# Attention and top-1 experts in one kernel: a new order for the first and last pairs of heads and the first expert block, and probabilities kept in two tiles

## The chip, the cores and the metric

The kernel runs on one core of a Trainium2 chip. The metric is the device time of one execution in microseconds. The profile is one profiled execution of the program. Engines are called as in the profile: PE is the matrix engine TensorE, PEld its weight loads, DVE is VectorE, ACT is ScalarE, POOL is GpSimd, and SP is the queue that issues most transfers.

## The reference

Attention over 8 batches of 8 heads, 576 tokens of 64 elements, with rotary embedding of q and k; its output, 4608 rows of 512, goes through a layer of eight experts of which each row uses one:

```python
scores = scale * np.matmul(q_rot, k_rot.transpose(0, 1, 3, 2))
scores = scores - np.max(scores, axis=-1, keepdims=True)
attn = np.exp(scores)
attn = attn / (np.sum(attn, axis=-1, keepdims=True) + 1e-09)
return np.matmul(attn, v).astype(np.float32)
...
x = np.ascontiguousarray(attn_out.transpose(0, 2, 1, 3)).reshape(B * S, H * D)
...
logits = x @ w_gate + modality_bias[modality_id]
e_idx = np.argmax(logits, axis=1)
...
gate_w = probs[np.arange(N), e_idx]
for e in range(E):
    mask = e_idx == e
    h = np.maximum(x[mask] @ w1[e], 0.0)
    out[mask] = gate_w[mask, None] * (h @ w2[e])
```

The experts' weights are 512 x 1024 and 1024 x 512, all in float32.

## The kernel before

**Attention.** The 64 heads are worked off as 32 pairs, four pairs to a batch. The steps of a pair are small jobs, and each has a name. T1, T2, R and LO are the rotary products (function `rope_`, L428 to L436, on POOL from the third pair on; HI, between R and LO, is a copy on ACT); SWH and SWL are transfers that swap the halves of partitions (L444, on SP). S0 to S8 are the scores on PE (L459), MN0 to MN8 the row extremes on DVE (L468), EX0 to EX8 the exponentials on ACT (L477), which write the probabilities. F0 to F3, FA and FB turn the probabilities over on PE (`fill`, L482), and A_ and B_ copy the result out of PSUM on ACT and DVE (`evac`, L419 and L516) into PH, and the tails of the sequence into PD. AVA and AVB multiply with v (L542): AVA for queries 0 to 255, AVB for queries 256 to 575. OTA and OTB copy that to SBUF, OUT multiplies with the gate's weights and turns it back (L577), and EVA and EVB (L589, L591, L593, on DVE) scale by the reciprocal row sum and write the rows X, the gate's logits G and the last 64 tokens XT. RE and RI prepare that reciprocal.

**Routing.** After each fourth pair BIAS, XO (the batch's rows go to DRAM) and fifteen steps RK0 to RK14 find each row's expert and its place in a table, and SC0 to SC4 write these places by indirect transfers from POOL (L694, `TAB<-VAL,oi`). A first plan (`plan0`, nine steps on POOL and DVE) assigns eight blocks of 256 rows from the first five batches alone, so that the experts' work can begin before attention is through.

**Experts.** For a block, SP reads the plan's values and the table (`ix`, `xi`), POOL works out addresses (L948) and issues eight indirect gathers (L956, `XG<-X,iy`), each of 128 rows of 128 elements. There are two buffers: even blocks use XG[0], odd blocks XG[1]. DVE transposes the rows (L1001, "tr"), ACT and DVE split them into a high and a low part in HL ("te"). The weights come by SP into staging buffers ST, and ACT (L419, W1H, W2H) and DVE (L416, W1L, W2L) split them in the same way ("hi", "lo"; "w1n", "hi2" and "lo2" are W1 for block 1). The first layer ("l1", L1020) is four groups of 24 matmuls, each of which fills one PSUM tile of half a slot; ACT (L1029, SW) and DVE (L1030, HX) read them ("l1e"). The second layer is L1043, ACT scales it (L1046), and POOL scatters it to the output (L1048).

**What sets the order.** Every job has a number. It is KEYS[name] + 14.438 x pair number, unless the table EDGE has an entry for that pair and name; jobs of the first expert block have theirs in the table MOE, relative to the last pair. All jobs are sorted by it, and the instructions of each engine and of SP's queue then run in exactly that order. Slot numbers for PSUM tiles (SLOTS) are fixed by name. From number 25 behind the last pair on, the expert blocks follow in a fixed program: block 0's second layer, block 1's first layer and so on, with the last batch's routing and the second plan woven in. The table AFTER adds waits ("place") to single gathers: gathers 3 to 7 of slot 0 wait for pair 30's AV or OUT, and all eight of slot 1 for slot 0's first layer. Waits between instructions otherwise follow from the tiles that they read and write; a PSUM tile of two halves counts as one.

Of the kernel before, what the change touches and what calls it, by code (L numbers as in the profile page):

```python
# [8 lines left out]
F32 = mybir.dt.float32  # L9
# [9 lines left out]
P = 128  # L19
# [43 lines left out]
        -329.744, "AVA": -327.201, "OTA": -302.117, "F3": -299.875, "A_F3": -295.073, "B_F3": -294.953, "AVB": -234.674, "OTB":  # L63
        -230.718, "RI": -224.645, "OUT": -153.228, "EVA": -132.782, "EVB": -119.484,
    },
# [1279 lines left out]
```

## Time and profile before

| | us |
|---|---|
| median of 3 runs | 931.47 (927.24 to 935.71) |
| profiled execution | 919.6 |
| its span | 917.8 |
| PE busy | 859.2 (94%) |
| DVE, ACT, POOL busy | 684.9, 631.3, 652.8 |
| mean granted TensorE clock | 0.983 |

The difference between 919.6 and 917.8 lies outside the recorded span. Attention fills the span up to about 470 us, the experts the rest. The strips of the page divide the span into 40 slices of 22.9 us, and a digit is the busy share in tenths. In a row of a timeline stand the start, the duration, engine, line, operation, output and inputs, the shape, and in brackets the idle time before it with what ended it; numbers of buffers are left out there (XG is either of the two). In the chain of waits stand start, duration and what the end of the program waited for at that time.

### The profile page before, as it was taken

How to read it: one execution, taken by the hardware profiler on the slowest of the kernel's cores; microseconds unless marked ns; L12 is line 12 of the kernel's file. 1: busy time of each engine (PE TensorE's matmuls, PEld its weight loads, DVE VectorE, ACT ScalarE, POOL GpSimd, SP SyncE). 2: the span in 40 equal slices, each digit the busy share in tenths (PEclk: the TensorE clock that was granted, in tenths of full speed). 3: DMA queues.
4: the chain of work that ended last, by engine and by line, in shares of the span. 5: the costliest groups of instructions: out<-in, count | busy, mean ns of one | idle time of the engine just before them, and what ended most of it. 6: DMA issues, size and time to landing. Idle time of an engine off the chain costs nothing.

```text
span 917.8 us, 25894 instructions
## 1 busy us (share of the span) xinstructions
PE 859.2 (94%) x9760; PEld 718.8 (78%) x9760; DVE 684.9 (75%) x1516; ACT 631.3 (69%) x1291; POOL 652.8 (71%) x494
## 2 busy tenths in 40 slices
PE   3899999999999999989994899999999999999995
PEld 2776777777777777766683799999999999999995
DVE  7777888888888889877781878766666666666662
ACT  2987988888988988978761555655555555555552
POOL 4989888998889899985466866766666666666400
PEclk9999999999999999999997799999999999999998
DMA  8776768978798887957612921127525112511240
GB/s 270 198 216 159 233 183 204 193 206 202 162 232 184 209 184 206 218 146 195 179 16 38 233 86 41 56 80 236 201 93 185 58 47 93 185 46 38 85 159 15
DMA packets 82466, 136.91 MB, mean 149 GB/s; under 512 B 28795, under 2 KB 53517, under 8 KB 81308
## 3 DMA queue, kind: packets, MB, share of 16 engines
q1 hardware_dynamic: 71740, 114.08, 47.2%
q0 software_dynamic: 9248, 19.46, 7.1%
q8 instruction: 79, 1.29, 0.6%
q10 hardware_dynamic: 1344, 1.62, 0.6%
q14 instruction: 55, 0.45, 0.2%
HBM read 138.16 MB, written 19.51 MB: 172 GB/s over the span
## 4 chain that ended last, share of the span: by engine, by line
PE 50%; issue 2%; POOL 1%; DVE 1%; DMA 1%; ACT 1%; POOLq 0%; DVEq 0%; ACTq 0%
PE psH L1020 22%; PE psY L1043 21%; PE ps L542 3%; PE ps L459 2%; PE ps L482 1%; POOL XG L956 1%; PE ps L1020 1%; DMA TAB<-VAL,oi 1%; PE ps L577 0%; DMA XG<-X,iy 0%; POOL TAB L694 0%; ACT PH L419 0%; DVE HL L416 0%; ACT P L477 0%; DVE X L589 0%
## 5 line engine op out<-in xcount | busy, mean ns | idle before, releaser
L477 ACT ACTIVATE P<-sc,mn 128x576 f32<-128x576 f32 x288 | 219.6, 766 | 5.9 <-DVE mn L468 4.8
L468 DVE CUSTOM_DVE_ANT_1 sc<-ps,ZERO 128x576 f32<-128x576 f32 x288 | 206.5, 748 | 21.8 <-PE ps L459 9.3
L1020 PE MATMUL psH<-HL,W1H 128*128 128x256 f32 x1152 | 205.2, 281 | 15.9 <-ACT W1H L419 15.9
L956 POOL DMA_INDIRECT XG<-X,iy x148 | 178.8, 1208 | 50.1 <-issue 36.7
L1020 PEld LDWEIGHTS psH<-HL,W1H 128*128 128x128 f32 x1152 | 178.9, 190 | 17.9 <-ACT W1H L419 16.4
L459 PE MATMUL ps<-SW 64*128 64x288 f32 x960 | 169.0, 311 | 14.7 <-DMA SW<-HL 12.5
L459 PE MATMUL ps<-HL 64*128 64x288 f32 x960 | 169.5, 311 | 5.8 <-DVE mn L468 2.1
L1020 PE MATMUL psH<-HL,W1L 128*128 128x256 f32 x576 | 162.1, 281 | 0.5 <-DVE W1L L416 0.5
L416 DVE TENSOR_TENSOR W1L<-ST,W1H 128x1024 fp32r<-128x1024 f32 x76 | 90.2, 1221 | 81.7 <-ACT W1H L419 81.6
L459 PEld LDWEIGHTS ps<-SW 64*128 64x128 f32 x960 | 135.5, 189 | 19.2 <-DMA SW<-HL 13.1
L459 PEld LDWEIGHTS ps<-HL 64*128 64x128 f32 x960 | 135.7, 189 | 11.3 <-issue 5.7
L542 PE MATMUL ps<-PH,V 128*64 128x320 f32 (+1 forms) x1024 | 138.2, 412 | 3.4 <-ACT P L477 2.1
L1048 POOL DMA_INDIRECT out_dram<-sc,ix x36 | 43.7, 1213 | 115.9 <-ACT sc L1046 100.0
L482 PEld LDWEIGHTS ps<-idf,P 64*128 64x128 f32 x2624 | 96.3, 139 | 33.3 <-ACT P L477 12.4
L1043 PE MATMUL psY<-W2L,SW 128*128 128x512 f32 (+1 forms) x304 | 118.0, 388 | 0.0
L1043 PE MATMUL psY<-W2H,SW 128*128 128x512 f32 (+1 forms) x304 | 116.7, 384 | 0.0
L482 PE MATMUL ps<-idf,P 64*128 64x64 f32 x2624 | 108.9, 226 | 7.5 <-ACT P L477 3.5
L516 DVE COPY PH<-ps 128x512 f32<-128x512 f32 (+1 forms) x160 | 98.4, 630 | 17.4 <-PE ps L482 12.2
L1020 PEld LDWEIGHTS psH<-HL,W1L 128*128 128x128 f32 x576 | 109.5, 190 | 0.8 <-DVE W1L L416 0.8
L436 POOL TENSOR_TENSOR HL<-ST,HL 128x1152 fp32r<-128x1152 f32 x31 | 82.4, 2657 | 38.9 <-ACT HL L419 38.8
L542 PEld LDWEIGHTS ps<-PH,V 128*64 128x64 f32 x1024 | 69.5, 136 | 50.3 <-issue 5.2
L419 ACT ACTIVATE PH<-ps 128x512 f32<-128x512 f32 (+1 forms) x160 | 85.5, 551 | 33.4 <-PE ps L482 25.4
(200 smaller groups left out, 1578.3 us busy)
## 6 DMA issues: line engine op xcount, KB each, us to landing
ST<-in_moe_w_dram SPq DMA_DIRECT2D x152, 512.0 KB
ST<-in_qk_dram SPq DMA_DIRECT2D x62, 576.0 KB
SW<-HL SPq DMA_DIRECT2D x124, 216.0 KB
V<-in_v_dram SPq DMA_DIRECT2D x32, 256.0 KB
X<-X SPq DMA_DIRECT2D x8, 1024.0 KB
XG<-X,iy POOLq DMA_INDIRECT x148, 3.1
V<-in_v_dram SPq DMA_DIRECT2D x64, 16.0 KB
X<-XT SPq DMA_DIRECT2D x16, 64.0 KB
```

What stands on the lines that cost most here:

```text
L416: nc.vector.tensor_tensor(o, a, b, op=ALU.subtract)
L419: return nc.scalar.activation(o, i, AF.Copy, scale=scale)
L436: e.tensor_tensor(d["HL"][:, 1, o], a, d["HL"][:, 0, o].bitcast(F32), op=ALU.subtract)
L459: nc.tensor.matmul(ps[:, g, 0:288], t[:, wq, q0:q0 + P], t[:, wk, k0:k0 + 288], start=(m == 0), stop=(m == len(L) - 1))
L468: nc.vector.tensor_tensor_reduce(sc, d.pop(("S", u))[:, :, 0:288], ZERO.unsqueeze(2).to_broadcast([P, 2, 288]), 1.0, FMAX, ALU.add, ALU.mi ...
L477: nc.scalar.activation(p, sc.rearrange("p a b -> p (a b)"), AF.Exp, bias=mn, scale=-1.0, accum_out=d["sum"][:, u:u + 1])
L482: nc.tensor.transpose(ps[:, g, c:c + 64], src[r, k0:k0 + P], idf[r, r])
L516: mine.append((nc.vector.tensor_copy if g else acopy)(o, i).ins)
L542: i = nc.tensor.matmul(pa[hh * 64:hh * 64 + 64, 0:c1 - c0], d["V"][:, hh, kt, :], r, start=(kt == 0), stop=(kt == 4))
L956: inst = nc.gpsimd.indirect_dma_start(out=XG[s % 2][:, t, g, :], out_offset=None, in_=X.rearrange("n (i f) -> (n i) f", f=P)[0:rows], in_o ...
L1020: l1_[s] = nc.tensor.matmul(ps[:, i, :], w[:, c, f0:f0 + P], x[:, c, :], start=(m == 0), stop=(m == 11)).ins
L1043: nc.tensor.matmul(ps, hx[:, c, t * P:(t + 1) * P], x[:, c, h * w:h * w + w], start=(m == 0), stop=(m == 23))
```

## The change

It has two parts.

**Tiles.** PH and PD, one tile each for all 576 queries, become two tiles each: index 0 for queries 0 to 255 and index 1 for queries 256 to 575. `evac` writes F0, F1 and FA into the first, F2, F3 and FB into the second, and `AV` reads the one of its half. PD is cleared by two instructions instead of one.

**Order.** The numbers of EDGE and MOE are new; KEYS, SLOTS and the period 14.438 stay. In EDGE pairs 0 and 1 keep their values but for the last three jobs of pair 1, pair 2 has nine new entries, pair 3 fifty, pairs 4 to 9 and 25 to 31 are new throughout, and pairs 19 and 23 have new numbers for routing and scatters. In MOE all rows are new but "setdma", "place" and "end" and the first five entries of "pl". AFTER is empty. The plan's last steps, the table reads and the first sixteen gathers come earlier, the gathers of slot 2 behind all of them; W2's loads come later, and W1's third quarter earlier. The first layer's groups run in the order 1, 2, 0, 3 instead of 1, 0, 3, 2.

```diff
 MOE = dict(
...
-    ix=(-13.525, 17.418, 11.679, 11.775),
-    w1=(-33.501, -27.735, 15.231, -22.655),
-    w2=(-4.011, 1.762, 12.647, -8.483),
+    ix=(-52.62160, -43.74680, -46.35270, 18.39360),
+    w1=(-23.84150, -10.48320, -23.09280, -25.00060),
+    w2=(18.46940, 16.92470, 15.40370, 5.88180),
...
-    l1=(17.301, 17.002, 22.720, 21.734),
+    l1=(20.38040, 19.40830, 19.49930, 23.70650),
...
-    PD = pp.tile([P, S], F32, name="PD")
+    PD = [pp.tile([P, n], F32, name=f"PD{i}") for i, n in enumerate((256, 320))]
...
-    PH = place(1, "ph").tile([P, 8, S], F32, name="PH")
+    ph = place(1, "ph")
+    PH = [ph.tile([P, 8, n], F32, name=f"PH{i}") for i, n in enumerate((256, 320))]
...
-        v_.memset(PD, 0.0)
+        for t in PD:
+            v_.memset(t, 0.0)
...
         if f[1] in "0123":
-            o = int(f[1]) * P + g * 64
-            cp(PH[:, :, o:o + 64], ps.rearrange("p (a b) -> p a b", b=64))
+            h, o = divmod(int(f[1]), 2)
+            o = o * P + g * 64
+            cp(PH[h][:, :, o:o + 64], ps.rearrange("p (a b) -> p a b", b=64))
             return
-        tails = PD[:, 0:512].rearrange("p (j s c) -> p j s c", s=2, c=64)[:, :, g, :]
+        tails = PD[f == "FB"][:, 0:256].rearrange("p (j s c) -> p j s c", s=2, c=64)[:, :, g, :]
         if f == "FA":
-            cp(tails[:, 0:2], ps[:, 0:128].rearrange("p (j c) -> p j c", c=64))
+            cp(tails, ps[:, 0:128].rearrange("p (j c) -> p j c", c=64))
         else:
-            cp(PH[:, 4 * g:4 * g + 4, 512:576], ps[:, 0:256].rearrange("p (k c) -> p k c", c=64))
-            cp(PD[g * 64:g * 64 + 64, 512:576], ps[g * 64:g * 64 + 64, 256:320])
-            cp(tails[:, 2:4], ps[:, 320:448].rearrange("p (j c) -> p j c", c=64))
+            cp(PH[1][:, 4 * g:4 * g + 4, 256:320], ps[:, 0:256].rearrange("p (k c) -> p k c", c=64))
+            cp(PD[1][g * 64:g * 64 + 64, 256:320], ps[g * 64:g * 64 + 64, 256:320])
+            cp(tails, ps[:, 320:448].rearrange("p (j c) -> p j c", c=64))
...
-                r = PH[:, 4 * hh + kt, c0:c1] if kt < 4 else PD[:, c0:c1]
+                r = PH[half][:, 4 * hh + kt, :] if kt < 4 else PD[half]
```

How the order changes is seen best on three engines. POOL, about the last batch's routing: XG_75 is XG[0], the rows of blocks 0 and 2, XG_76 is XG[1], the rows of block 1, and `TAB<-VAL,oi` is a scatter of places. Line numbers are 46 or 47 higher in the changed kernel. Before:

```order
L683 CAST oi<-of 128x5
L694 DMA TAB<-VAL,oi 41472x2 x2
L948 TENSOR_SCALAR iy<-xi,CF 128x8
L956 DMA XG_75<-X,iy 128x128
L694 DMA TAB<-VAL,oi 41472x2
L948 TENSOR_SCALAR iy<-xi,CF 128x8
L956 DMA XG_76<-X,iy 128x128
L956 DMA XG_75<-X,iy 128x128
L956 DMA XG_76<-X,iy 128x128 x2
L694 DMA TAB<-VAL,oi 41472x2
```

The last rope product of pair 31 (L436) stands fifteen rows above this piece. Afterwards, from that product on:

```order
L1003 DMA XG_76<-X,iy 128x128
L482 TENSOR_TENSOR HL_83<-ST_74,HL_83 128x1152
L1003 DMA XG_76<-X,iy 128x128
L722 TENSOR_TENSOR rk<-rk,OH 128x40
L682 TENSOR_TENSOR dl<-lg,mx 128x40
L684 TENSOR_SCALAR vv<-dl 128x40
L685 TENSOR_TENSOR vv<-vv,CF 128x40
L1003 DMA XG_76<-X,iy 128x128 x4
L694 TENSOR_TENSOR vv<-vv,vm 128x40
L695 TENSOR_SCALAR OH<-vv 128x32
L696 TENSOR_SCALAR OH<-vv 64x8
L1003 DMA XG_75<-X,iy 128x128 x6
```

Five gathers stand ahead of the last rope product (the last of them in the first row), and the other eleven among batch 6's routing steps, ahead of its scatters; no gather is left between scatters but slot 2's, which follow later.

PE, at the end of block 0's first layer: ps_126 and ps_125 before, ps_129, ps_128 and ps_130 afterwards, are PSUM tiles, oT_113 before and oT_114 afterwards belong to pair 31, oT_113 afterwards to pair 30. Before:

```order
L1020 MATMUL ps_126<-HL_82,W1H 128x256 x2
L1020 MATMUL ps_126<-HL_82,W1L 128x256
L577 MATMUL ps_125<-RW,oT_113 64x72 x18
L1043 MATMUL psY<-W2H,SW_84 128x512
L1043 MATMUL psY<-W2H,HX 128x512
```

And afterwards:

```order
L1067 MATMUL ps_129<-HL_82,W1H 128x256 x2
L1067 MATMUL ps_129<-HL_82,W1L 128x256
L624 MATMUL ps_128<-RW,oT_114 64x72 x18
L624 MATMUL ps_130<-RW,oT_113 64x72 x18
L1090 MATMUL psY<-W2H,SW_84 128x512
```

Pair 30's OUT has moved behind the first layer, to pair 31's.

DVE, in the same place: HX is the low part of the first layer's result, and X, G and XT are what a pair's evacuation writes. Before:

```order
L416 TENSOR_TENSOR W2L<-ST_74,W2H 128x1024
L677 RECIPROCAL VAL<-ee 128x5
L416 TENSOR_TENSOR W1L<-ST_73,W1H 128x4x256
L416 TENSOR_TENSOR W2L<-ST_74,W2H 128x1024
L1030 SCALAR_TENSOR_TENSOR HX<-ps_127,SW_84 128x512 x2
L589 TENSOR_TENSOR X<-ps_125,ri 128x4x2x32
L591 TENSOR_TENSOR G<-ps_125,ri 128x4x8
L593 TENSOR_SCALAR XT<-ps_125,ri 64x2x36
```

And afterwards:

```order
L1077 SCALAR_TENSOR_TENSOR HX<-ps_127,SW_84 128x512
L724 RECIPROCAL VAL<-ee 128x5
L1077 SCALAR_TENSOR_TENSOR HX<-ps_129,SW_84 128x512
L462 TENSOR_TENSOR W2L<-ST_74,W2H 128x1024
L636 TENSOR_TENSOR X<-ps_128,ri 128x4x2x32
L638 TENSOR_TENSOR G<-ps_128,ri 128x4x8
L640 TENSOR_SCALAR XT<-ps_128,ri 64x2x36
L462 TENSOR_TENSOR W2L<-ST_74,W2H 128x1024
```

The reads of the first two groups now go to two tiles with a step of routing between them, and pair 29's evacuation (ps_128) stands behind them, among W2's splits.

More of the change, by code (lines that the diff above doesn't have):

```diff
@@ L124 @@
+    8: {
+        "LD1": -97.34400, "LD": -93.21340, "T2": -78.16160, "T1": -76.89470, "R": -44.96430, "HI": -38.22990, "LO": -26.13570, "SWH":
+        -18.39730,
+    },
+    9: {
+        "LD": -74.37830, "LD1": -65.48030, "T1": -37.69560, "T2": -33.90710,
+    },
+    10: {
+        "LD1": -42.30700,
     },
     19: {
-        "SC3": 113.825, "SC2": 128.215, "SC4": 152.075,
+        "SC3": 98.84680, "SC2": 99.15330, "SC4": 100.50310,
     },
     23: {
-        "RK6": 45.016, "RK7": 49.391, "RK8": 52.824, "RK9": 58.160, "RK10": 79.988, "RK11": 109.721, "RK12": 128.347, "RK13": 128.956,
@@ L130 @@
-        "RK14": 129.684, "SC3": 130.859, "SC4": 132.359, "SC2": 132.942, "SC1": 136.961, "SC0": 137.506,
+        "RK4": 40.39880, "RK5": 45.38510, "RK6": 55.87350, "RK7": 58.30030, "RK8": 64.83020, "RK9": 66.86950, "RK10": 96.79000, "RK11":
+        104.00940, "RK12": 110.23510, "RK13": 130.84540, "RK14": 131.85820, "SC1": 138.55930, "SC3": 140.07750, "SC4": 140.17130, "SC0":
+        140.30170, "SC2": 140.37860,
+    },
+    24: {
+        "RI": 24.92530, "EVB": 27.33970, "EVA": 28.04020,
     },
@@ L132 @@
     25: {
-        "RE": 11.575, "F2": 13.246, "A_F2": 14.351, "B_F2": 14.486, "RI": 16.427, "AVB": 18.725, "OTB": 20.519, "OUT": 26.426, "EVB":
-        26.591, "EVA": 30.118,
+        "S4": 5.22290, "MN4": 7.36290, "EX4": 7.56740, "F2": 8.79190, "A_F2": 10.08970, "FB": 10.09500, "B_F2": 10.25040, "AVA":
+        12.00140, "B_FB": 12.33000, "A_FB": 13.35490, "F3": 13.67210, "OTA": 14.17460, "A_F3": 14.54600, "B_F3": 14.59550, "RE":
+        16.00560, "AVB": 17.42890, "OTB": 19.54030, "RI": 24.93540, "OUT": 29.24800, "EVB": 30.88160, "EVA": 31.77910,
@@ new lines @@
+        13.72270, "A_FB": 13.80310, "B_F2": 13.84600, "OTA": 14.98000, "B_FB": 16.97510, "AVB": 18.53230, "RI": 19.72150, "OTB":
+        20.93250, "OUT": 29.11230, "EVB": 30.23300, "BIAS": 30.42580, "EVA": 30.58860, "RK0": 37.77770, "RK1": 46.47540, "XO": 49.60010,
+        "RK2": 50.23090, "RK3": 50.63790, "RK4": 52.37830, "RK5": 57.02010, "RK6": 63.94850, "RK7": 66.12590, "RK8": 72.30630, "RK9":
+        73.69750, "RK10": 74.24720, "RK11": 74.75730, "RK12": 78.59730, "RK13": 80.58540, "RK14": 82.27160, "SC0": 83.07400, "SC1":
@@ L154 @@
+        83.17400, "SC2": 83.27400, "SC3": 83.37400, "SC4": 83.47400,
     },
     28: {
[6 rows of a table removed]
-        "OTA": 17.939, "RE": 19.181, "AVB": 20.414, "OTB": 23.398, "RI": 25.977, "OUT": 38.336, "EVA": 39.257, "EVB": 40.186,
[7 rows of a table added]
+        "AVA": 16.58290, "OTA": 17.32300, "AVB": 23.17150, "OTB": 24.93340, "RI": 28.15800, "OUT": 42.31590, "EVB": 44.88510, "EVA":
+        46.04530,
     },
     29: {
[6 rows of a table removed]
-        "B_FB": 12.181, "OTA": 12.576, "RE": 12.876, "B_F3": 13.074, "RI": 13.187, "A_F3": 13.894, "AVB": 15.303, "OTB": 20.667, "OUT":
@@ L192 @@
-        23.807, "OUT": 24.531,
[7 rows of a table added]
+        12.26820, "A_FB": 12.59160, "A_F3": 13.10210, "AVB": 13.27550, "OTA": 18.43940, "OTB": 19.76400, "OUT": 23.97810, "RE":
+        24.60040, "BIAS": 24.81490,
     },
@@ L209 @@
-    l1e=(22.809, 22.869, 24.662, 24.647),
-    w1n=(20.502, 24.643, 23.254, 22.825),
-    place=(10.490, 11.490),
-    rows=(5.189, -7.595, 2.778, 1.170, -0.984, 8.071, 5.429, 11.766, 24.719, 23.818, 21.468, 24.323, 19.920, 20.117, 22.957, 17.444,
-        18.250, 23.228, 17.169, 21.813, 22.941, 24.907, 21.508, 22.829),
-    pl=(-114.356, -102.856, -99.906, -88.406, -85.506, -73.956, -51.417, -48.907, -45.303),
+    setdma=(-353.06960, -199.65400, -64.08250, -129.15640),
+    consts=(-29.61450, -5.23550),
@@ new lines @@
+    plan=(-64.54160, -81.13280, -67.04820, 14.99810),
+    ix=(-52.62160, -43.74680, -46.35270, 18.39360),
+    w1=(-23.84150, -10.48320, -23.09280, -25.00060),
+    w2=(18.46940, 16.92470, 15.40370, 5.88180),
+    hi=(7.92200, -3.40500, 16.39520, 13.66060),
+    lo=(14.56510, 9.32750, 19.34950, 20.36720),
+    tr=(13.24560, 12.38010),
+    te=(13.90720, 13.67560),
+    hi2=(22.09220, 19.80050, 18.48590, 14.23580),
+    lo2=(22.55070, 21.82130, 19.57480, 20.45140),
+    l1=(20.38040, 19.40830, 19.49930, 23.70650),
@@ new lines @@
+    l1e=(23.22350, 20.66810, 21.16750, 24.07900),
+    w1n=(19.17720, 12.22160, 23.75970, 23.16240),
+    place=(10.49000, 11.49000),
+    rows=(7.75000, 8.92180, -35.72320, 10.31500, 6.63150, 6.86200, 9.13200, -40.78360, -13.64720, 4.00060, -19.59050, 4.02450, 0.82960,
+        -20.94490, 3.34560, -33.77170, 25.12200, 25.13200, 25.14200, 25.15200, 25.16200, 25.17200, 25.18200, 25.19200),
+    pl=(-114.35600, -102.85600, -99.90600, -88.40600, -85.50600, -85.04670, -81.96580, -81.33250, -81.19150),
@@ L215 @@
     end=25.0,
 )
-AFTER = {(0, 3): (30, 'av', 0), (0, 4): (30, 'av', 0), (0, 5): (30, 'av', 1), (0, 6): (30, 'av', 1), (0, 7): (30, 'out', 1), (1, 0): ('l1', 0), (1, 1): ('l1', 0), (1, 2): ('l1', 0), (1, 3): ('l1', 0), (1, 4): ('l1', 0), (1, 5): ('l1', 0), (1, 6): ('l1', 0), (1, 7): ('l1', 0)}
+AFTER = {}
 PIN = "PE,Activation,DVE,Pool"
```

48 lines of the change are left out of this document (23 added, 25 removed), and 174 rows, old and new, of the table EDGE.

## The prediction

> **What bounds the kernel now.** I read the page's slices first, then a table of windows, then the chain of waits at the joint of the two halves, and last the timelines of single engines there. The two strips of the page give TensorE's busy tenths and the clock granted to it in 40 slices of 22.9 us.
>
> ```profile
> PE   3899999999999999989994899999999999999995
> PEclk9999999999999999999997799999999999999998
> ```
>
> The strips have three weak places: the first slices, the slices about 400 us, and the one at 500 us, where the clock falls too. The table of windows puts numbers on them; its columns are the stretch, its length, busy time and count of each engine, then granted clock, share of the 16 DMA engines and GB/s.
>
> ```profile
> core 0: us, PE busy (x) PEld busy (x) DVE busy (x) ACT busy (x) POOL busy (x), PEclk, DMA share, GB/s
> 0.00:30.00 30.00, 12.34 (x126) 10.30 (x126) 22.61 (x55) 12.87 (x28) 16.83 (x26) 0.95 0.85 267
> 30.00:100.00 70.00, 66.38 (x1044) 51.73 (x1046) 55.12 (x158) 57.60 (x146) 62.56 (x39) 1.00 0.69 203
> 100.00:390.00 290.00, 287.19 (x4710) 219.52 (x4710) 250.48 (x756) 256.96 (x662) 263.52 (x171) 1.00 0.82 197
> 390.00:470.00 80.00, 71.39 (x1127) 53.84 (x1122) 61.91 (x171) 63.46 (x157) 47.58 (x50) 1.00 0.55 151
> 470.00:492.40 22.40, 22.40 (x173) 19.81 (x172) 11.77 (x21) 5.47 (x9) 18.68 (x14) 1.00 0.25 28
> 492.40:509.60 17.20, 0.85 (x3) 0.50 (x2) 7.29 (x15) 5.26 (x8) 11.80 (x13) 0.57 0.54 85
> 509.60:523.60 14.00, 13.97 (x101) 13.93 (x102) 11.41 (x20) 7.85 (x11) 11.51 (x10) 0.80 0.85 203
> 523.60:908.00 384.40, 384.40 (x2496) 349.05 (x2495) 264.35 (x326) 221.39 (x274) 219.30 (x176) 1.00 0.33 105
> 908.00:917.80 9.80, 0.30 (x3) 0.09 (x1) 0.00 (x0) 0.47 (x1) 0.98 (x1) 0.66 0.09 31
> ```
>
> So TensorE is the bound: idle 2.8 us of 290 in the middle of attention and not at all from 523.6 to 908. A new order can win there next to nothing. What it can win is 17.7 us of idle time at the start, 3.6 up to 100, 8.6 between 390 and 470, 16.4 from 492.4 to 509.6, and the slow clock behind that hole. The chain of waits shows what fills the hole:
>
> ```profile
> 468.97 5.82 PE ps L1020 x48
> ...
> 489.02 5.16 DMA TAB<-VAL,oi
> ...
> 498.23 2.56 DMA XG<-X,iy
> ...
> 500.92 0.72 DVE XG L1001
> ...
> 507.26 1.06 ACT W1H L419
> ...
> 508.35 1.24 DVE W1L L416
> ...
> 509.63 8.15 PE psH L1020 x46
> ...
> ...
> 523.64 11.10 PE psY L1043 x48
> 534.74 11.20 PE psH L1020 x96
> ```
>
> Block 0's first layer begins at 468.97. Block 1's rows are not in the chip until its last gather, issued at 498.23 after a row of gathers and scatters on POOL, has landed at 500.8. The transposes, the splits of the rows and of W1's first quarter follow, and block 1's first layer begins only at 509.63. It then takes 14.0 us up to 523.64, where block 2's took 11.20: the clock.
>
> **The gathers.** POOL's timeline in that place:
>
> ```profile
> 456.18 1.01 POOL L956 DMA_INDIRECT XG<-X,iy  x1 [0.30 <-issue]
> ...
> 470.94 5.23 POOL L694 DMA_INDIRECT TAB<-VAL,oi  x1 [0.31 <-issue]
> ...
> 479.54 2.57 POOL L956 DMA_INDIRECT XG<-X,iy  x1 [0.30 <-issue]
> ```
>
> Before, slot 1's eight gathers wait for block 0's first layer ("place"), and block 2's rows, which go to the same buffer as block 0's, are mixed between them. Afterwards all sixteen gathers of slots 0 and 1 stand ahead of pair 31's last route steps, with no place waits, and slot 2's eight come after everything. At the 1.0 us and the gap of 0.3 of the first row they are 16 × 1.3 = 21 us of POOL time, moved from both sides of 470 to well ahead of it. POOL is busy 47.6 of 80 us between 390 and 470, so there is room. The gathers drop out of the chain, and the question is what is late next.
>
> **Block 0, then block 1, step by step.** Counted from the start of block 0's first layer, at t = 0. Each of its four groups is a quarter of 11.2, so 2.8. Groups 1, 2 and 0 run to 8.4. Group 3 goes into the same PSUM tile as group 2 and must wait until group 2 has been read, and the read of group 1 itself waits for group 0, which shares its tile. The rows of such a read:
>
> ```profile
> 474.81 0.60 ACT L1029 ACTIVATE SW<-ps 128x512 fp32r<-128x512 f32 x1 [2.33 <-PE ps L1020]
> 476.16 0.60 ACT L1029 ACTIVATE SW<-ps 128x512 fp32r<-128x512 f32 x1 [0.76 <-DVE HX L1030]
> 475.44 0.69 DVE L1030 SCALAR_TENSOR_TENSOR HX<-ps,SW 128x512 fp32r<-128x512 f32 x1 [0.16 <-ACT SW L1029]
> 469.12 0.41 DVE L589 TENSOR_TENSOR X<-ps,ri 128x256 f32<-128x256 f32 x1
> 469.96 0.42 DVE L589 TENSOR_TENSOR X<-ps,ri 128x256 f32<-128x256 f32 x1
> 470.60 1.21 DVE L416 TENSOR_TENSOR W1L<-ST,W1H 128x1024 fp32r<-128x1024 f32 x1
> 474.07 1.21 DVE L416 TENSOR_TENSOR W2L<-ST,W2H 128x1024 fp32r<-128x1024 f32 x1
> 480.30 0.86 PE L577 MATMUL ps<-RW,oT 64*64 64x72 f32 x36
> 481.08 0.50 PE L1043 MATMUL psY<-W2H,SW 128*128 128x512 f32 x1
> ```
>
> 0.60 + 0.69 + 0.69 with the hand-overs lies between 2.0 and 2.7 (474.79, where the matmuls end, to 476.76 + 0.69); I take 2.35. Group 3 then runs from 10.75 to 13.55. OUT.31 writes the tile that pair 29's evacuation reads, and DVE does two W2L splits (1.21 each) and two evacuations (469.12 to 469.96, 0.84 each) ahead of that: 10.75 + 4.1 = 14.85, a gap of 1.3. OUT.31 and OUT.30 take 0.8 each (480.30 to 481.08), and block 0's second layer runs from 16.5 for 11.1 us, to 27.6. Before, it began at 12.1 (481.08 − 468.97): the order at this place costs 4.4.
>
> What block 1 needs: pair 30's two evacuations up to 18.2, then what the chain shows from 500.92 to 509.63, all of it the same work (transpose, splits, pair 31's evacuation, W1's first quarter): 8.7, so ready at 26.9. That is 0.7 before TensorE is free at 27.6: the hole closes, with little to spare. Block 1's first layer then runs for 11.2 and ends at 38.8, where before it ended at 523.64 − 468.97 = 54.7: 15.9 won, of which 2.8 are the clock.
>
> Against that stand the two new gaps of 2.35 and 1.3. The nearest row for what such a gap does to the clock is at the start:
>
> ```profile
> 25.74 0.47 PE L482 MATMUL ps<-idf,P 64*128 64x64 f32 x8 [1.91 <-ACT P L477]
> 28.00:30.00 2.00, 2.00 (x24) 1.83 (x20) 1.24 (x2) 1.40 (x4) 2.00 (x1) 0.50 0.90 254
> ```
>
> A wait of 1.91 us was followed, two microseconds later, by a granted clock of 0.50. The 2 us shown at half speed cost 1.0; with what lies ahead of and behind the window I take 1.6, once: 14.3 left. The ends are 0 and, for both gaps, 3.2.
>
> [...]
>
> **The attention half.** The new keys of pairs 4 to 9 and 25 to 31 change the order and add no instruction, but for one clearing of PD. Pairs 0 to 2 run nearly as before, so the 17.7 us of the start stay; what can move is 3.6 (up to 100) and 8.6 (390 to 470), 12.2 together. Two rows price the other side, the rope products of the last pairs on POOL, which the first gathers are now put between:
>
> ```profile
> 413.81 2.65 POOL L436 TENSOR_TENSOR HL<-ST,HL 128x1152 fp32r<-128x1152 f32 x1
> 431.17 2.67 POOL L436 TENSOR_TENSOR HL<-ST,HL 128x1152 fp32r<-128x1152 f32 x1 [4.73 <-ACT HL L419]
> ```
>
> Five gathers stand ahead of pair 31's last one (the 431.17 row): 5 × 1.3 = 6.5 us, beside three scatters that stood there already. POOL waited 4.73 before it, so the gathers fit unless they are stretched. I take 3 us won, a quarter of 12.2, between −4 (the gathers' 6.5 less most of that slack, and some late scores) and +8.
>
> The two tiles by query half let the first AV begin without the second half's copies, and the next pair's copies start when the first AV is through. These waits stand in the table of waits:
>
> ```profile
> DVE PH L516 <- PE ps L542: 4.7, 3, 2.0
> ACT PH L419 <- PE ps L542: 3.6, 2, 2.3
> ```
>
> Five waits over 32 pairs, on engines that are not the bound: worth at most the 2.8 idle us of the middle, and I count it inside the 3. The later loads of W2 are hidden beside block 0's first layer, with the DMA engines a quarter busy from 470 to 492; if that cover is gone, the second layer slips by what a split costs, 1.2 us. The plan's earlier steps and the earlier table reads are small POOL and SP work and cost nothing on TensorE; on SP's queue the loads that stand behind them are for later pairs.
>
> **The sum.** 14.3 + 3 = 17.3 of 917.8: a span of 900.5, with the 1.8 us outside it 902.3. The median of the runs shown is 931.47 against 919.6 for the profiled run, 1.0129 of it, so 914.
>
> **The rivals.** *Everything closes.* The gaps of the ends go as well: 16.4 + 2.8 + 8.6 = 27.8 won, 891.8, as a median 903. For it speaks that every one of these idle stretches is a wait and none a shortage of an engine; against it, that the order after block 0's groups makes two new waits.
>
> *New waits take half.* Block 1's preparation has 0.7 us to spare. If pair 31's evacuation or the W1 copy comes 5 us late, or a hole above 3 us brings the slow clock back for the whole of a first layer (2.8), and the last pairs win nothing, then 7 are left: 910.8 + 1.8, a median of 924. For it speaks that DVE and ACT do all of it in one chain; against it, that each piece was measured in this very place.
>
> *Slower, by stretched gathers.* The scatter at 470.94 took 5.23 us where its kind takes 1.0, and it lay beside five weight splits on DVE back to back (470.60 to 475.28); the gather at 479.54 took 2.57 beside two more. If the eight indirect transfers now ahead of pair 31's rope product all took 5.2, POOL would be 8 × 4.1 = 33 us late, 28 beyond the slack of 4.7. TensorE waits for that rope product, so the span would be 900.5 + 28 and the median 943. It decides from about 22 us late on, 3.9 us a transfer. Against it stands the gather at 456.18, which took 1.0 beside a reduction that DVE reads out of PSUM:
>
> ```profile
> 455.94 0.75 DVE L468 CUSTOM_DVE_ANT_1 sc<-ps,ZERO 128x576 f32<-128x576 f32 x1
> ```
>
> And ahead of pair 31's rope product DVE's work is mostly of that kind: nine such reductions a pair and the copies out of PSUM, with the splits behind them.
>
> [...]
>
> *The hole stays.* If block 1 really waits for its weights' transfers rather than for its rows, the gathers' move wins nothing: 931. The chain's W1H copy at 507.26 waited for ACT's order and not for a transfer, which speaks against it.
>
> **How the numbers follow.** The forecast of 914 has 0.57, with an own range of 907 to 922 (attention from −4 to +8 us, clock from 0 to 3.2); everything closes 0.15; new waits 0.16; slower 0.08; the hole stays 0.04. 1% of 931.47 is 9.3 us, about what a measurement of this kernel can tell from no change. Faster by more than that, under 922.2: 0.56 + 0.15 + 0.02 = 0.73. Within it: 0.01 + 0.14 + 0.04 = 0.19. Slower: 0.08. The range from 902 to 927 leaves out the slow case, the unchanged one and the edges of the others.
>
> **What would show it.** In the changed profile, TensorE's longest idle time between block 0's second layer and block 1's first should be under 1 us, and the clock 1.00 there; the chain should run there through matmuls, with no gather and no scatter in it. Two waits of about 2.4 and 1.3 us should stand about group 3 and OUT.31, and a stretch of granted clock near 0.5 soon behind them. The last rope product should begin at about 430. It is wrong if a gather among the last ropes takes over 3 us, if a wait of TensorE above 3 us stands before the last pairs' scores, or if a hole of over 3 us is left ahead of block 1, with the split of its rows or weights as its releaser.

## The result and the profile after

The changed kernel takes 935.01 us (median of 20 runs, 930.73 to 938.17), the kernel before 927.14 in the same set of runs (922.89 to 935.71): a ratio of 1.0077 (1.0057 to 1.0098). It is 0.8% slower, where 914 us and a range of 902 to 927 were forecast. The profiled execution has a span of 933.8 us at a mean granted clock of 0.98, against 917.8 before.

One thing has to be known ahead of the experiments: sets of runs, each on one chip at one time, differ by more than the change is worth. The kernel before took 919.3 to 920.9 us in three of the sets below and 926.6 to 929.0 in the other three and in the record's, and the changed kernel 909 in one and 935 to 943 in the others. Every ratio here is taken within its set, and from the fast runs alone, so it is not always the ratio of the two medians.

The strips of the page of the changed kernel, TensorE's busy tenths and its granted clock in 40 slices:

```profile
PE   3899999999999999899688999999999999999995
PEclk9999999999999999999887999999999999999998
```

The weak place is no longer the one slice at 500 us; it lies earlier and is wider, the three slices from about 443 to 514. The table of windows, with the columns as in the prediction:

```profile
100.00:390.00 290.00, 280.57 (x4582) 215.34 (x4578) 245.83 (x736) 248.98 (x642) 259.54 (x179) 1.00 0.80 194
390.00:470.00 80.00, 66.78 (x977) 50.28 (x979) 53.40 (x156) 57.14 (x146) 57.34 (x45) 0.92 0.57 161
470.00:500.00 30.00, 26.73 (x316) 20.89 (x313) 20.07 (x36) 18.36 (x35) 5.99 (x3) 0.94 0.15 54
500.00:540.00 40.00, 37.90 (x267) 32.62 (x266) 28.78 (x58) 17.25 (x25) 21.54 (x22) 0.87 0.50 152
540.00:924.00 384.00, 381.84 (x2471) 346.12 (x2470) 259.75 (x319) 218.27 (x270) 224.99 (x183) 1.00 0.31 101
```

TensorE is idle for 13.2 us between 390 and 470 (8.6 before) and 9.4 between 100 and 390 (2.8 before), and the clock is below 1.00 from 390 to 540. The chain of waits through block 0 and the joint:

```profile
456.25 2.99 another core or an unknown queue
...
460.75 4.37 another core or an unknown queue
...
468.24 4.53 PE ps L589 x20
...
488.64 8.53 PE ps L1067 x72
...
499.23 4.23 PE ps L1067 x24
503.46 1.44 PE ps L624 x48
...
509.69 13.31 PE psY L1090 x47
523.00 5.59 PE psH L1067 x48
...
534.46 11.20 PE psY L1090 x48
```

Block 1 is ready when TensorE is: its first layer starts at 523.00, right behind block 0's second, and no gather or scatter is left in the chain. But block 0 begins at 488.6 where it began at 468.97, and there is a releaser that the chain before did not have, "another core or an unknown queue", for 7.4 us in the two pieces shown. The span is made up so, by the timeline's starts: the first layer of block 0 is 19.6 later (488.5 against 468.9); from it to the end of block 1's first layer 45.8 in place of 54.6, 8.8 won; from there to the end 399.5 in place of 394.3, 5.2 lost. 19.6 − 8.8 + 5.2 = 16.0, the difference of the spans. So the joint did close, and it was more than paid for before and behind it.

The unknown releaser in the timelines of ACT, DVE and PE of the changed kernel; the bracket holds the idle time before the instruction and what ended it, and "remote" is an event of which the trace has no sender:

```profile
459.27 0.60 ACT L465 ACTIVATE PH<-ps 128x512 f32<-128x512 f32 x1 [3.02 <-remote]
465.13 0.77 ACT L523 ACTIVATE P<-sc,mn 128x576 f32<-128x576 f32 x1 [4.39 <-remote]
```

```profile
466.57 0.42 DVE L562 COPY PH<-ps 128x256 f32<-128x256 f32 x1 [5.61 <-remote]
```

```profile
461.46 0.38 PE L528 MATMUL ps<-idf,P 64*128 64x64 f32 x2 [0.22 <-issue]
468.24 2.37 PE L589 MATMUL ps<-PH,V 128*64 128x256 f32 x9 [6.40 <-ACT P L523]
```

DVE copies what PE's L528 matmuls left in PSUM. By the trace the last of these ended at 461.84 (461.46 + 0.38); the copy was let go at 466.57, 4.7 us later. No record is missing that could explain it: the trace holds 9760 matmuls, as the one before does. PE then had nothing to do for 6.4 us, and the granted clock is 0.50 for 13.7 us from 459.8 on.

### The profile page after: what moved, and what is told of

Read it like the earlier page. It is cut to its first block, busy times and chain, and to the rows that moved or that the text cites. A ratio compares the mean times of both kernels' runs of the same rounds, so it can differ in the third digit from the quotient of the medians.

```text
span 933.8 us, 25892 instructions
## 1 busy us (share of the span) xinstructions
PE 872.4 (93%) x9760; PEld 725.9 (78%) x9760; DVE 686.9 (74%) x1517; ACT 631.8 (68%) x1291; POOL 647.1 (69%) x494
## 2 busy tenths in 40 slices
DMA packets 82466, 136.91 MB, mean 147 GB/s; under 512 B 28795, under 2 KB 53517, under 8 KB 81308
## 4 chain that ended last, share of the span: by engine, by line
PE 82%; ACT 6%; issue 2%; DVE 2%; another core or an unknown queue 1%; POOL 0%; POOLq 0%; ACTq 0%; DVEq 0%
PE psY L1090 22%; PE psH L1067 22%; PE ps L589 15%; PE ps L505 11%; PE ps L528 8%; ACT P L523 3%; PE ps L624 3%; PE ps L1067 1%; ACT PH L465 1%; DVE PH L562 0%; DVE lg L677 0%; DVE PD L562 0%; ACT oT L465 0%; DVE sc L514 0%
## 5 line engine op out<-in xcount | busy, mean ns | idle before, releaser
L1067 PE MATMUL psH<-HL,W1H 128*128 128x256 f32 x1152 | 203.1, 279 | 0.6 <-issue 0.4
L1067 PEld LDWEIGHTS psH<-HL,W1H 128*128 128x128 f32 x1152 | 176.9, 188 | 2.8 <-issue 1.1
L589 PE MATMUL ps<-PH,V 128*64 128x320 f32 (+1 forms) x1024 | 141.7, 419 | 14.9 <-ACT P L523 6.7
L528 PEld LDWEIGHTS ps<-idf,P 64*128 64x128 f32 x2624 | 96.1, 139 | 33.9 <-issue 12.9
L589 PEld LDWEIGHTS ps<-PH,V 128*64 128x64 f32 x1024 | 71.9, 139 | 62.0 <-ACT PH L465 8.6
L528 PE MATMUL ps<-idf,P 64*128 64x64 f32 x2624 | 108.9, 226 | 7.7 <-ACT P L523 4.0
## 6 DMA issues: line engine op xcount, KB each, us to landing
ST<-in_moe_w_dram SPq DMA_DIRECT2D x152, 512.0 KB
```

The lines of the kernel that those rows point to most:

```text
L528: nc.tensor.transpose(ps[:, g, c:c + 64], src[r, k0:k0 + P], idf[r, r])
L589: i = nc.tensor.matmul(pa[hh * 64:hh * 64 + 64, 0:c1 - c0], d["V"][:, hh, kt, :], r, start=(kt == 0), stop=(kt == 4))
L1067: l1_[s] = nc.tensor.matmul(ps[:, i, :], w[:, c, f0:f0 + P], x[:, c, :], start=(m == 0), stop=(m == 11)).ins
```

## The experiments

### First set: tiles, start and end apart

My theory at that point was that the end of the order (pairs 25 to 31 and the first block) made TensorE late; the rivals were the tiles and the start (pairs 3 to 9). `tiles_only` is the changed code with the order of before (the tables of numbers fill pages, so where the edit is in them the fence says it in words):

```diff
-EDGE, MOE, AFTER: the new numbers
+EDGE, MOE, AFTER: the numbers of before
```

> The changed kernel's two tiles for PH and PD with the order tables of before (EDGE, MOE, AFTER). Theory: the loss is in the order alone and the tiles free a few waits on engines that are not the bound, so 0.997 to 1.002 of before. Rival: the two tiles themselves slow the steady middle, whose 17 pairs between the tenth and the twenty-seventh took 2 us longer in the changed profile; then 1.002 to 1.006, and the middle shows it.

Measured: 927.53, ratio 1.0005 (0.9977 to 1.0032). The two tiles are worth nothing. `order_only` is the other half, one tile each as before and all the new numbers:

```diff
-    PD = [pp.tile([P, n], F32, name=f"PD{i}") for i, n in enumerate((256, 320))]
+    PD = pp.tile([P, S], F32, name="PD")
...
-                r = PH[half][:, 4 * hh + kt, :] if kt < 4 else PD[half]
+                r = PH[:, 4 * hh + kt, c0:c1] if kt < 4 else PD[:, c0:c1]
```

> The new order tables with PH and PD as one tile each, as before. Theory (the order makes the loss): 1.005 to 1.015, no better than the changed kernel's 1.008, since without the second tile the first AV has more copies to wait for. Rival (the tiles make it): 0.995 to 1.003.

Measured: 937.03, 1.0089 (1.0061 to 1.0117). All of the result is the order's. `start_only` has the new entries of EDGE up to pair 9 and the two constants of MOE, all else as before; `end_only` has the reverse, the new entries of pairs 19, 23 and 25 to 31 and the new MOE:

```diff
-EDGE[0..9], MOE["consts"]: the numbers of before (start_only) / new (end_only)
+EDGE[0..9], MOE["consts"]: new (start_only) / the numbers of before (end_only)
```

> Two tiles, the new numbers of pairs 0 to 9 and of the two constants' jobs, everything else as before. In the changed profile the tenth rope product was 3.8 us later than before. Theory: this part costs those 3 to 4 us, 1.003 to 1.005. Rival: the 3.8 us lie within the scatter of single executions (the profile of before was 7.5 us under its median), then 0.998 to 1.002.

> Two tiles, the numbers of pairs 0 to 9 and of the constants as before, and the new ones of pairs 19 and 23 to 31, of the first block and the gathers. Theory: here lies most of it. The hole ahead of block 1 closes (about 9 us won in the changed profile, up to 16), the last pairs lose more (about 14 us between the rope product of pair 26 and block 0's first layer) by waits of AV for probabilities, with the half clock behind each: 1.003 to 1.008. Rival: the end wins on balance and the start loses it, then 0.990 to 0.998.

Measured: 931.41, 1.0040 (1.0016 to 1.0064), and 931.65, 1.0043 (1.0017 to 1.0069). Each half costs 0.4%. For the start the table of windows shows where. In the kernel before:

```profile
100.00:145.00 45.00, 44.88 (x756) 34.09 (x756) 38.71 (x121) 40.15 (x104) 37.89 (x21) 1.00 0.65 172
```

In start_only the same work lasts up to 148.8:

```profile
100.00:148.80 48.80, 46.30 (x766) 34.70 (x764) 38.41 (x118) 39.18 (x103) 40.46 (x22) 1.00 0.66 180
```

TensorE is idle for 2.5 us there, in place of 0.1. The table of waits of PE in start_only, 30 to 148.8 us, names small ones that the table of before, 30 to 145, doesn't have (here L341 is the scores, L425 the products with v):

```profile
PE ps L341 <- ACT PD L301: 1.2, 1, 1.2
PE ps L425 <- DVE XT L476: 0.8, 1, 0.8
```

The rope products show the sum: pair 9's starts at 131.5, before at 127.8, and from there to pair 19 they run 3.7 to 4.3 us later than before; 3.8 of 928 is the 0.4%. (Behind pair 19 the trace falls further back, to 7.7 at pair 31; tiles_only, from the same set, is 1.8 behind there too.) In the end's half, the joint closed and the time did not fall.

### Second set: the gathers, the block and the pairs apart

`gathers_only` has the two tiles, and the old order but for the plan, the table reads, the rows and the entries of pairs 19 and 23 that these need, with AFTER empty:

```diff
 MOE = dict(
...
-    plan=(-34.727, 16.183, -5.857, -25.884),
-    ix=(-13.525, 17.418, 11.679, 11.775),
+    plan=(-64.5416, -81.1328, -67.0482, 14.9981),
+    ix=(-52.6216, -43.7468, -46.3527, 18.3936),
...
-    rows=(5.189, -7.595, 2.778, 1.170, -0.984, 8.071, 5.429, 11.766,
+    rows=(7.75, 8.9218, -35.7232, 10.315, 6.6315, 6.862, 9.132, -40.7836,
...
```

> Two tiles and the order of before, but the plan's steps, the table reads, the routing of pairs 19 and 23 and all gathers at the new numbers, without place waits. Theory A, the sixteen early gathers slow the last pairs themselves (in three profiles with them ACT and DVE wait 3 to 7 us for results of PE that its records show as done, from about 456 us on, and the half clock follows for 13.7 us): block 0's first layer starts 6 to 10 us later than before, the hole ahead of block 1 closes to under 3 us, ratio 0.990 to 1.000. Theory B, the new order of pairs 25 to 31 does it: the first layer starts within 2 us of before and the hole closes, ratio 0.980 to 0.988.

Measured: 904.91 against 920.92, 0.9831 (0.9798 to 0.9865). The gathers alone win 1.7%. The chain of gathers_only through the joint, where L902 is the first layer, L459 the OUT matmuls and L925 the second layer:

```profile
471.79 11.40 PE ps L902 x96
483.19 0.79 PE ps L459 x36
483.97 11.30 PE psY L925 x48
495.27 5.59 PE psH L902 x48
```

Both layers of block 0 and block 1's first follow on each other without a gap. Block 0 starts 2.8 us later than before (471.7). `block_only` adds the rest of the new MOE (the weights' loads and splits, the order of block 0's groups, W1 for block 1), with the pairs as before:

```diff
-    w2=(-4.011, 1.762, 12.647, -8.483),
+    w2=(18.4694, 16.9247, 15.4037, 5.8818),
...
-    l1=(17.301, 17.002, 22.72, 21.734),
-    l1e=(22.809, 22.869, 24.662, 24.647),
+    l1=(20.3804, 19.4083, 19.4993, 23.7065),
+    l1e=(23.2235, 20.6681, 21.1675, 24.079),
...
```

> Two tiles and the order of before for all pairs (routing of 19 and 23 new), with the whole new table of the first block: gathers, loads, splits, first layer in the order 1, 2, 0, 3. Against the gathers alone it shows what the block's own new order costs: by the changed profile block 0's second layer begins 20.5 us after its first instead of 12.2, so 0.5 to 1% more than the gathers alone; if the order of the block is harmless without the new pairs, within 0.2% of it.

Measured: 912.58, 0.9908 (0.9876 to 0.9939), which is 0.9908 / 0.9831 = 1.0078 of gathers_only. The block's own order takes back about half of what the gathers win. TensorE's timeline in block_only has the two waits that the prediction saw in the order, ahead of group 3 and of OUT:

```profile
483.85 0.50 PE L902 MATMUL ps<-HL,W1H 128*128 128x256 f32 x2 [2.01 <-DVE HX L912]
...
488.34 0.86 PE L459 MATMUL ps<-RW,oT 64*64 64x72 f32 x36 [1.42 <-DVE XT L475]
```

Block 0's second layer begins 16.8 us after its first, in gathers_only 12.2. `late_gathers` is end_only with the gathers' numbers of before:

```diff
-    rows=(7.75, 8.9218, -35.7232, 10.315, 6.6315, 6.862, 9.132, -40.7836,
+    rows=(5.189, -7.595, 2.778, 1.17, -0.984, 8.071, 5.429, 11.766,
...
```

> Two tiles, pairs 0 to 9 as before, the new order of pairs 19 and 23 to 31 and of the block, but the gathers at their old numbers, without place waits. Theory A: no late results of PE and no half clock at about 458 us, block 0's first layer starts 6 to 10 us earlier than the 486.5 of the run with the new end, and the hole ahead of block 1 is back with 10 to 17 us: ratio 1.000 to 1.012. Theory B: the late results and the half clock stay at about 456 to 471 us, the hole comes on top, ratio 1.012 to 1.025.

Measured: 923.78, 1.0031 (1.0010 to 1.0052); block 1's first layer begins at 511.9, later still than before (508.4 by the same reading of the timeline). So the new pairs and the new block without the early gathers win nothing.

### Third set: which gathers, and the tiles again

The riddle was now that the gathers won 1.7% in gathers_only, while end_only, which has them too, lost 0.4%. The suspects were the five gathers between the last rope products, the tiles and one slot's gathers. `gathers_behind` moves those five behind the ropes:

```diff
-    rows=(7.75, 8.9218, -35.7232, 10.315, 6.6315, 6.862, 9.132, -40.7836, -13.6472, 4.0006, -19.5905, 4.0245, 0.8296, -20.9449, 3.3456, -33.7717,
+    rows=(7.75, 8.9218, -13.3, 10.315, 6.6315, 6.862, 9.132, -13.9, -13.6472, 4.0006, -11.5, 4.0245, 0.8296, -12.1, 3.3456, -12.7,
...
```

> As the run with the gathers alone, but the five gathers that stood between the last rope products now stand right behind the last of them. In that run the rope products of pairs 27 to 31 came 3 to 7 us later than before and block 0's first layer 2.8 us later. Theory (five gathers on POOL's queue make that delay): first layer back to 469 to 470, ratio 0.978 to 0.982. Rival (the gap in the last pairs has other owners, or the sixteen gathers then end too late for block 0): 0.983 to 0.988.

Measured: 906.03 against 919.74, 0.9844 (0.9818 to 0.9870), the same as gathers_only. Block 0's first layer starts at 474.3, not at 469 to 470: the five gathers on POOL's queue weren't what made it late. `gathers_1tile` has gathers_only's numbers in the code of before, with PH and PD as one tile each.

> The gathers alone, with PH and PD as one tile each, as before. Theory (the tiles are worth nothing, as with the old gathers): 0.981 to 0.986, the same as with two tiles. Rival (with the hole closed the tiles win 2 to 4 us): 0.986 to 0.990.

Measured: 905.95, 0.9843 (0.9818 to 0.9868): again the tiles do nothing. `end_slot1` and `end_slot0` are end_only with the early gathers of slot 1 or of slot 0 alone:

```diff
-    rows=(7.75, 8.9218, -35.7232, 10.315, 6.6315, 6.862, 9.132, -40.7836,
+    rows=(5.189, -7.595, 2.778, 1.17, -0.984, 8.071, 5.429, 11.766,
...
```

(this is end_slot1; end_slot0 puts the old numbers in the other sixteen places).

> The run with the new end, but slot 0's eight gathers at their old numbers (slot 1's at the new ones, no place waits). POOL still has some ten gathers in a row behind the last rope product. Theory C, the late results of PE come from a long row of gathers beside the new order of the last pairs: they stay, the half clock at about 457 lasts over 10 us, the first layer starts at 482 to 488. Rival, they hang on where single gathers stand among the ropes and routing: they go or shrink, the first layer starts at 470 to 476.

> The run with the new end, but slot 1's eight gathers at their old numbers (slot 0's at the new ones, no place waits). Behind the last rope product stand six of slot 0's in a row, and slot 1's come later. Theory C: the row of six is shorter and earlier, so late results shrink to under 3 us and the first layer starts at 470 to 478. Rival: they stay as they are, first layer at 482 to 488. In both cases a hole of 3 to 15 us ahead of block 1.

One profiled execution each: 904.9 and 921.6. Neither trace has late results of PE, and block 0's first layer starts at 468.1 and 469.0; theory C failed in the first, its rival in the second. Slot 1's gathers carry the gain, since block 1's first layer starts at 495.4 with them and at 511.2 without. With block_only's 0.9908 from the other set, end_slot1's 904.9 / 919.74 = 0.984 points to some 0.7% that the new order of pairs 25 to 31 wins back; that rests on one execution, on two sets, and on kernels that differ in slot 0's gathers too, so it isn't shown.

### Fourth set: the same four kernels side by side

From these numbers the culprit of the loss would have been slot 0's eight gathers, since end_only and end_slot1 differ in them alone. But the two stood in different sets. So changed kernel, end_only, end_slot1 and gathers_only were run again, unedited, in one set.

> The changed kernel itself once more, beside the others of this set. Theory D, its late results of PE (456 to 468 us, 503 to 509, 578 to 583) come from outside the program and were there in the first set of runs alone: ratio 0.985 to 0.995, block 0's first layer starts at 471 to 476. Theory E, they belong to the program (its place of slot 0's gathers): ratio 1.005 to 1.010 as before, first layer at 486 to 490.

> The run with the new end once more. Theory D: 0.980 to 0.990, first layer at 467 to 472. Theory E: 1.002 to 1.008, first layer at 484 to 488, half clock for 13.7 us at about 457.

> The new end with slot 0's gathers at their old numbers, now timed. One look gave 904.9 beside 919.7 of before. Theories D and E alike: 0.982 to 0.988; under D the run with the new end stands within 0.3% of it, under E 1.5% and more above it.

> The gathers alone, with the order of before elsewhere, once more, so that all four are compared on the same chip in the same hour. 0.981 to 0.987 by either theory.

Measured, against 929.01: changed kernel 943.43, 1.0148 (1.0111 to 1.0185); end_only 937.23, 1.0079 (1.0044 to 1.0113); end_slot1 940.35, 1.0119 (1.0075 to 1.0162); gathers_only 932.19, 0.9984 (0.9950 to 1.0017; without its runs of 939.1 and 4699.64 its median is 929.8). That ends the theory about slot 0: end_slot1 is no better than end_only. Theory D fell too, and gathers_only missed the 0.981 to 0.987 that both theories gave it. The same program, byte for byte, took 904.9 and 940.4 (end_slot1), 904.9 and 929.8 (gathers_only), while the kernel before went from 920 to 929. I call the sets and traces in which it takes 919 to 921 the early kind, the others the late kind. The table of waits of gathers_only's second run, 340 to 490 us, has what the first run has nowhere:

```profile
ACT PH L300 <- remote: 6.2, 3, 2.7
DVE PH L397 <- remote: 6.1, 2, 3.7
```

Block 0's first layer starts at 488.8 in it, at 471.7 in the first. The two kinds can be told apart by another row. The last part of the page gives, behind the comma, the median time from issue to landing. Of gathers_only's gathers, in its first run and in its second:

```profile
XG<-X,iy POOLq DMA_INDIRECT x148, 3.1
```

```profile
XG<-X,iy POOLq DMA_INDIRECT x148
```

The page has that time in all nine traces of the early kind, the profile of the kernel before in the record among them, and in none of the eleven of the late kind. What it means isn't known.

### Fifth and sixth set: the changed kernel again

The question was whether these late releases belong to the changed program, which so far had always shown them. The changed kernel and the kernel before ran together, and the changed kernel again later.

> The changed kernel once more in another set of runs. Theory F: its loss needs two things, its many indirect transfers ahead of block 0 and a state of the chip in which PE's instructions come in steps of 0.74 us beside them; sets differ in that state, and before shows it by 927 to 929 us instead of 920. Where before measures 918 to 922 here, the changed kernel stands at 0.985 to 0.993 (the new end's 0.984 with its start's 0.004); where before measures 926 to 930, at 1.005 to 1.016. Theory E, the loss belongs to the program: 1.005 to 1.016 in both.

> The kernel before, for its own trace in this set. Theory F: in a set where before takes 926 to 930 its trace too has stretches behind 380 us in which PE's matmuls come in bursts 0.74 us apart and half clock behind them, 5 to 10 us in all, and no hole of another length; in a set with 918 to 922 none.

Measured: 935.13 against 926.62, 1.0093 (1.0062 to 1.0124); the profiled execution of the kernel before has a span of 925.1, and in it three such waits, 9.9 us in all, where its profile in the record has none. The first of them stands at 531, behind the joint:

```profile
ACT SW L1029 <- remote: 3.0, 1, 3.0
```

Its first layer of block 0 starts at 474.9, 6.0 later than in the record's trace and ahead of all three. The bursts of PE, 0.74 us apart, that theory F expected in it are not there.

> The changed kernel in a further set of runs. Theory F: beside a before of 918 to 922 it stands at 0.985 to 0.993, with block 0's first layer at 471 to 476 and no late results of PE; beside a before of 926 to 930 at 1.005 to 1.016. Theory E, the loss belongs to the program: 1.005 to 1.016 beside either.

Measured: 909.05 against 919.26, 0.9868 (0.9835 to 0.9901). The late releases do not belong to the program: here the changed kernel is 1.3% faster, at a clock of 1.00 throughout the joint. Its windows:

```profile
390.00:470.00 80.00, 74.24 (x1172) 57.10 (x1170) 62.11 (x177) 63.83 (x163) 55.85 (x45) 0.98 0.62 169
...
500.00:540.00 40.00, 40.00 (x274) 36.57 (x274) 31.05 (x53) 23.92 (x31) 30.73 (x25) 1.00 0.52 170
```

And its chain at the joint:

```profile
473.35 8.52 PE ps L1067 x72
...
481.90 0.61 ACT SW L1076
...
482.53 0.53 DVE HX L1077
...
483.31 0.57 DVE HX L1077
...
487.90 1.48 PE ps L624 x70
489.38 11.30 PE psY L1090 x48
500.69 5.59 PE psH L1067 x48
```

The parts, taken from the sets where the kernel before took 919 to 921, add up: gathers and block and last pairs 0.984 (end_slot1, one execution, with slot 0's gathers late), start +0.004 (from the first set, which is of the late kind), tiles 0, together 0.988, against 0.9868 measured. As two of these terms come from other conditions, the sum agrees with the result and doesn't prove its parts.

The version that came out best is gathers_only: 0.9831 where the changed kernel later had 0.9868, and 0.9984 where it had 1.0148.

## Why the prediction was wrong

**The joint: right in the sixth set's trace, 7.0 short in the record's.** Counted from the start of block 0's first layer, 38.8 us were forecast up to the end of block 1's; the sixth set's trace has 512.0 − 473.2 = 38.8. The second layer starts at 16.1 (forecast 16.5). The two waits about group 3 and OUT.31, forecast as 2.35 and 1.3, are in the table of groups, 430 to 500 us, of that trace:

```profile
L1067 PE MATMUL ps<-HL,W1H 128*128 128x256 f32 x64 | 11.5, 282 | 2.1 <-DVE HX L1077 2.1
...
L624 PE MATMUL ps<-RW,oT 64*64 64x72 f32 x144 | 3.2, 227 | 0.9 <-DVE of L727 0.9
```

The second is put down to a step of routing that stands right behind the evacuation on DVE. The hole is gone without a wait: the second layer ends at 489.38 + 11.30 = 500.68, block 1's first starts at 500.69. In the record's trace the same stretch took 45.8; the 7.0 more are the slower matmuls and the OUT matmuls in pieces that the last section shows. gathers_only adds that the 4.4 us that I charged to the order of block 0 were avoidable: the early gathers don't need it.

**The clock after the gaps: off by 1.6 in one trace, right in the other.** In the sixth set's, a wait of 2.1 was followed by a clock of 1.00. In the record's trace, TensorE's timeline behind the wait of 2.08:

```profile
499.23 0.50 PE L1067 MATMUL ps<-HL,W1H 128*128 128x256 f32 x2 [2.08 <-DVE HX L1077]
...
500.39 0.40 PE L1067 MATMUL ps<-HL,W1H 128*128 128x256 f32 x2
...
501.34 0.63 PE L1067 MATMUL ps<-HL,W1H 128*128 128x256 f32 x2
```

The same two matmuls take 0.40 and, a microsecond later, 0.63: the clock is at 0.50 for 3.4 us, from 500.8. So the length of the wait alone does not decide it here: 2.1 was followed by 1.00 and 2.08 by 0.50, and a third one, of 1.77 us ahead of 438.98 in the sixth set's trace, lies in 15 us (430 to 445) with a mean clock of 0.89. The record's trace of before has 3.4 us at half clock behind the wait of 1.91 (from 27.1) and 20.5 about the hole (from 494.7); that of the changed kernel has 3.4, 13.7, 3.4, 6.8 and 3.4 (from 391.6, 459.8, 500.8, 507.6 and 582.7). What decides whether such a stretch comes, and how long it is, these traces don't show. By an estimate from these rows 3.4 us at half speed cost 1.7, close to the 1.6 taken; of the two waits ahead of group 3, 2.08 was followed by that and 2.1 by nothing, and which it would be was luck in either trace.

**Attention, 3 us won: this step failed, in sign and in kind.** Where nothing came late, in the sixth set, block 0 began 4.3 us later than before (473.2 against 468.9), just beyond the lower end of −4. The start, pairs 3 to 9, accounts for it: in that trace pair 9's rope product starts at 132.3, 4.6 later than before, pair 26's is 4.7 later, and its table of waits up to 149 has the same short waits as start_only's. I had counted the idle time of before as what could be won and had not asked what short waits the new order would make there. The last rope product came at 433.1, forecast 430. In the record's trace block 0 began 19.6 us later; no row of the profile of before had such a wait, and the range had no room for it. In the sixth set the terms make up the span, 907.5 against 900.5 forecast: 4.3 + 3 by attention, 1.6 less by the clock, and 1.2 behind the joint (395.5 in place of 394.3), 6.9 of the 7.0. In the record's trace the span is 33.3 over the forecast: 22.6 by attention (3 won forecast, 19.6 lost), 5.5 at the joint with its clock, and 5.2 behind it, where TensorE stands idle for 2.2 us, mostly from 579 to 583, and 3.4 us at half clock follow, from 582.7.

**The step to the median: failed.** The profiled execution of before (919.6) was of the kind of sets in which that kernel takes 919 to 921, and the three runs beside it (median 931.47) of the other. The landing times of its gathers, shown above, say the same. I carried the difference over as a factor, 1.0129, as if it were the same for any order. It is not: between the two kinds, before gains 0.9%, gathers_only 2.7% (929.8 against 904.9) and the changed kernel 2.9 to 3.8% (935.1 and 943.4 against 909.05). That 909.05 lies in the range of 902 to 927 is in part luck: its profiled execution took 909.28, so that set needs no such factor, and the same terms without it give 902.3. Against a trace of the kernel before of the same kind, before_c, the changed kernel of the record reads: first layer 488.5 against 474.9, 13.6 lost, of which 4.3 are the order's by the sixth set, and the other 9.3 I put down to the late releases and the slow matmuls behind them, by subtraction; joint 45.8 against 54.2, 8.4 won; rest 399.5 against 396.0, 3.5 lost; 8.7 in all, 0.9%.

**The rivals.** *Stretched gathers* named the right sign, and the instructions whose early place goes with the loss, with a wrong mechanism. The gathers between the last ropes, on POOL in the sixth set's trace:

```profile
432.07 1.02 POOL L1003 DMA_INDIRECT XG<-X,iy  x1 [0.16 <-issue]
433.12 2.67 POOL L482 TENSOR_TENSOR HL<-ST,HL 128x1152 fp32r<-128x1152 f32 x1
```

They took 1.0 to 1.1 us here and in the record's trace of the changed kernel, and gathers_behind, without them there, gained the same. *Everything closes* fell by the two waits and the start. *New waits take half* (924) was not it either: block 1 was never late. *The hole stays* is refuted by 500.68 and 500.69.

**What stays open** is why TensorE's results come late in some sets. It isn't the program (after_d), the tiles (order_only has one tile each and 29 us of such waits), or one chip (the first and the third set ran on the same one, and the kernel before took 927.42 and 919.74 there). The record's two traces, before of the early kind and after of the late one, have the same number of transfers' packets (82466) and, among them, of fetches of instructions (79 and 55); the landing times of the gathers are what differs (3.1 us in the first page, none in the second). That kernels with the early gathers lose more by it, the times say: between the two kinds of sets gathers_only differs by 2.7%, the kernel before by 0.9%, and the gathers' gain of 1.7% shrinks to 0.2%. The traces of the late kind agree: by their tables of waits TensorE's OUT matmuls stand for 2.5 to 7.5 us on nothing that the profile shows ("issue") in all eight of kernels with early gathers, and not at all in before_c, tiles_only and start_only. The new pairs and block without the early gathers (late_gathers) never ran in a set of the late kind. How the gathers do it isn't known.

## What to carry to other kernels

A stall that the chain names as a transfer's order can be priced step by step and won by moving that transfer alone, here 1.7% in the sets of the early kind and next to nothing (0.2%) in the one of the late kind; what came along with it (a new order of the block and of the first pairs) cost 0.8% and 0.4%. The idle time of TensorE in the kernel before is not what a new order can win: ask first which short waits it makes. Before two experiments from different sets are set against each other, run one of them again in the other's set: a whole theory about slot 0's gathers rested on such a pair, and fell when the same two programs stood side by side.

## What the hardware showed that was not expected

In the record's trace of the changed kernel TensorE issues in bursts 0.74 us apart for some microseconds, while POOL issues indirect transfers. OUT's matmuls on PE, of which 70 took 1.48 in the sixth set's chain:

```profile
505.26 0.38 PE L624 MATMUL ps<-RW,oT 64*64 64x72 f32 x4 [0.36 <-issue]
506.01 0.36 PE L624 MATMUL ps<-RW,oT 64*64 64x72 f32 x4 [0.37 <-issue]
506.75 0.36 PE L624 MATMUL ps<-RW,oT 64*64 64x72 f32 x5 [0.38 <-issue]
```

And POOL in the same microseconds:

```profile
505.29 0.93 POOL L741 DMA_INDIRECT TAB<-VAL,oi  x1 [0.30 <-issue]
506.52 0.99 POOL L741 DMA_INDIRECT TAB<-VAL,oi  x1 [0.30 <-issue]
```

Four or five matmuls run, then TensorE stands for 0.37 us on nothing that the profile shows. The same scatters run from 488.69 on in the sixth set's trace, beside block 0's second layer, and TensorE has no such gaps there, so they are not enough by themselves. And one scatter of gathers_only took 5.23 us again, as that at 470.94 did before, with four weight splits beside it on DVE, from 473.54 to 478.22. POOL's row, and the second of the splits:

```profile
473.85 5.23 POOL L576 DMA_INDIRECT TAB<-VAL,oi  x1 [0.30 <-issue]
```

```profile
474.67 1.22 DVE L297 TENSOR_TENSOR W2L<-ST,W2H 128x1024 fp32r<-128x1024 f32 x1
```

In both places a scatter that otherwise takes 0.9 to 1.1 us lasts 5.23 beside four weight splits with a reciprocal among them (before, 470.60 to 475.28); the gathers among the last ropes, at 1.0 to 1.1 us, show nothing of it. Whether the splits are the cause isn't shown.
